# Decode attention on one core: K's sums all on DVE in blocks of 64 keys, V a head behind K

## The chip, the core and the metric

The kernel runs on one core of a Trainium2 chip. The metric is the device time of one execution in microseconds (us). Here it is the median of three runs, 1392.78 us (1392.25 to 1393.84). The profile is of one further execution.

The core has several engines that run side by side: PE (matrix multiply, TensorE), DVE (VectorE), ACT (ScalarE), POOL (GpSimd) and SP (SyncE, which here only issues DMA transfers). Transfers between the chip's main memory and the core's on-chip buffers are carried by 16 DMA engines, which all queues share. A tile lies across 128 partitions; PSUM is the memory that PE writes its results to.

## The reference

One token is decoded. It is normalised, goes through an attention over a cache of 16384 keys for each of 32 heads, and beside that through a gated feed-forward part:

```python
xn = _layernorm(x)                                   # x: 576 numbers
q = (xn @ wq) as 32 heads of 128
scores = einsum("bhqd,bhkd->bhqk", q, k_cache) * 128 ** -0.5
p = softmax(scores)                                  # over 16384 keys
o = einsum("bhqk,bhkd->bhqd", p, v_cache)
A = o as a row of 4096 @ wo
B = (gelu(xn @ w_gate) * (xn @ w_up)) @ w_down       # 4608 wide
return x + A + B
```

All is float32. One head's K is 16384 x 128 numbers, 8.39 MB, and its V the same, so that the 32 heads bring 537 MB; the weights wq, w_gate, w_up, w_down and wo bring some 51 MB more. Every byte is used once.

## The kernel before, in words

**Layout.** Partition p holds 128 keys of a head (R = 128) with 128 numbers each, so one head's K or V is one tile of 128x16384, 64 KB in each partition, loaded by one DMA from SP. Three such buffers, `slots` (L41), are all that fits; `slot()` (L57) hands them out in turn, and a load waits until the last reader of the tile that was there before is done. The loads of weights, K and V all go through `load` (L60), so they stand in SP's queue in the order of the program, and a load that waits holds up those behind it.

**Start.** One slot, `mix`, takes the tails of wq, w_gate and w_up and their fourth rows; wq has a slot of its own. `project` (L121) multiplies xn with a weight on PE, in four groups of partitions. `ffn` (L153) loads the rest of w_gate or w_up into a slot, projects, lets ACT copy the result into that slot's unused end (`gc`, L160), and four small DMAs from POOL's queue gather it into `gu` (L164). `ffn_act` (L171) then computes gelu(g) * u into `hT`, on DVE with one tanh on ACT; its last DVE operation (L181) waits for the gathers of w_up's part.

**A head.** `q_spread` (L143) puts the head's q on all partitions. `qk` (L192) does 16 keys of every partition at a time, 8 times: DVE multiplies K in place with q (L198), DVE then sums 10 of the 16 keys' products (L202), and ACT sums the other 6, each with one activation that also accumulates (L201, which the profile shows as an ACTIVATE and a READ_ACCUMULATOR). `softmax` (L204) finds the largest score: a maximum on DVE (L206), a transpose on PE (L208), a maximum on DVE again (L210), a matmul that puts it on all partitions (L212); ACT then takes exp (L216). `pv` (L218) multiplies V with the probabilities in 32 matmuls of four keys, which the profile shows as 64; the four keys' results stand in four rows and four blocks of PSUM, of which only the matching ones (row r, block r) are wanted. `out_a` (L225) picks these on DVE, with a multiplication by a mask in PSUM (L227) and a sum (L229), and `out_b` (L231) sums the partitions on PE (L233). The picking for head h-1 stands behind the fourth block of head h.

**Order of the loads.** K0, V0, K1, V1 and so on through the three slots. So K of head h+1 takes the slot of V of head h-1 and waits for its PV; V of head h takes the slot of K of head h-1 and waits for its sums. Between engines the order is set by a scheduler that goes by the program's order where the program does not pin it with `keep_in_program_order`.

**End.** w_down comes in pieces of 28 and 8 rows of 576 numbers per partition (L265, L266), wo in pieces of 20, 6, 3, 2 and 1 rows (L267 to L271). The attention output is divided by the sums of exp and gathered into `oT` by a DMA (L289). `add_out` (L255) multiplies each row of w_down with hT and each row of wo with oT, accumulating in PSUM (L258); from row 26 of wo on (MERGE) two of the four partial sums are folded into the other two (L303, L305). Then x is added (L309) and the result stored (L310).

Of the kernel before, what the change touches and what calls it, by code (L numbers as in the profile page):

```python
# [16 lines left out]
R = SK // P  # L17
SUB = 16
NSUB = R // SUB
N_ACT = 6  # L20
SLOTS = 3
DJ = 4
# [4 lines left out]
HD = H * DH  # L27
QG, QB = HD // 4, 512
FG, FB = DF // 4, 384
WD_T = DF // P  # L30
WO_T = HD // P
WD_PIECES = (28, 8)
WO_PIECES = (20, 6, 3, 2, 1)
MERGE = 26
# [3 lines left out]
def kernel(ctx: ExitStack, tc: tile.TileContext, x, k_cache, v_cache, wq, wo, wg, wu, wd, out):  # L38
    nc = tc.nc
    cpool = ctx.enter_context(tc.tile_pool(name="cpool", bufs=1))  # L40
    slots = ctx.enter_context(tc.tile_pool(name="slots", bufs=SLOTS))  # L41
    spool = ctx.enter_context(tc.tile_pool(name="spool", bufs=2))
# [13 lines left out]

    def slot():  # L57
        return slots.tile([P, R * DH], F32, tag="s", name="slot")

    def load(dst, src):  # L60
        nc.sync.dma_start(dst, src)
        return dst

    mix, wq_t = slot(), slot()
    at = 0

    def part_of_mix(src):
        nonlocal at
        n = src.shape[1]
        at += n  # L70
        return load(mix[:, at - n : at], src)

    ROW3 = 3 * DF
    tails = {"q": part_of_mix(wtail["q"])}
    load(wq_t, wmain["q"])
    row3 = {}
    for n in "gu":
        row3[n] = part_of_mix(wmain[n][:, ROW3:])
        tails[n] = part_of_mix(wtail[n])

# [26 lines left out]
    for j in range(DJ):  # L107
        nc.tensor.matmul(px[:, j : j + 1], xm[:, j, :], ones[:1, :1], start=True, stop=True)
    xd = cpool.tile([1, D - DM, 2], F32, name="xd")
    nc.vector.tensor_copy(xd, xrow[:, DM:].unsqueeze(2).to_broadcast([1, D - DM, 2]))  # L110
# [24 lines left out]

    steps = [(DJ, tails["q"])] + [(j, wq_t[:, j * HD : (j + 1) * HD]) for j in range(DJ)]
    pq = project(steps, QG, QB)
# [15 lines left out]
    def ffn(which):  # L153
        n = "gu"[which]
        t = slot()
        steps = [(3, row3[n]), (DJ, tails[n])]
        for j in range(DJ - 1):
            lo, hi = j * DF, (j + 1) * DF
            steps.append((j, load(t[:, lo:hi], wmain[n][:, lo:hi])))
        gc = t[:, ROW3 : ROW3 + FG]  # L160
        pg = project(steps, FG, FB)
        nc.scalar.activation(gc.rearrange("p (b f) -> p b f", f=FB), pg, AF.Copy)
        for q in range(4):
            nc.gpsimd.dma_start(gu[32 * q : 32 * q + 32, which, :], gc[32 * q : 32 * q + 1, :])  # L164
# [22 lines left out]

    S, PE_, KT, VT, OM = {}, {}, {}, {}, {}
    lsum = cpool.tile([P, H], F32, name="lsum")
    oall = cpool.tile([P, H], F32, name="oall")  # L190

    def qk(h, i):  # L192
        kt = KT[h].rearrange("p (n d) -> p n d", d=DH)
        if i == 0:
            S[h] = spool.tile([P, R], F32, name="s")
        lo, nv = i * SUB, SUB - N_ACT
        blk = kt[:, lo : lo + SUB, :]
        nc.vector.tensor_mul(blk, blk, Q[h].to_broadcast([P, SUB, DH]))  # L198
        for n in range(nv, SUB):
            jk = spool.tile([P, DH], F32, name="jk", bufs=1)  # L200
            nc.scalar.activation(jk, blk[:, n, :], AF.Copy, accum_out=S[h][:, lo + n : lo + n + 1])  # L201
        nc.vector.tensor_reduce(S[h][:, lo : lo + nv], blk[:, :nv, :], axis=AX.X, op=ALU.add)  # L202

    def softmax(h):  # L204
        pm = spool.tile([P, 1], F32, name="pm")
        nc.vector.reduce_max(pm, S[h], axis=AX.X)  # L206
        pt = ps_s.tile([P, 512], F32, tag="sm", name="pt")
        nc.tensor.transpose(pt[:1, :P], pm, ident)  # L208
        nm = spool.tile([1, 1], F32, name="nm")
        nc.vector.tensor_reduce(nm, pt[:1, :P], axis=AX.X, op=ALU.max, negate=True)  # L210
# [5 lines left out]
        nc.scalar.activation(PE_[h], S.pop(h), AF.Exp, bias=nb, scale=SCALE, accum_out=lsum[:, h : h + 1])  # L216

    def pv(h):  # L218
        vt, pe = VT.pop(h), PE_.pop(h)
        for k in range(0, R, 4):  # L220
            q = 32 * (k // 4 % 4)
            nc.tensor.matmul(PO[h % 2][q : q + 4, :], pe[:, k : k + 4], vt[:, k * DH : (k + 4) * DH],  # L222
                             start=k < 16, stop=k >= R - 16)
# [12 lines left out]
    q_spread(0)  # L236
    for h in range(H):
        KT[h] = load(slot(), kv[h])
        VT[h] = load(slot(), vv[h])
        for i in range(NSUB):  # L240
            qk(h, i)
            if h == 0 and i == 3:
                ffn_act()
            if h > 0 and i == 3:
                out_a(h - 1)
                out_b(h - 1)
        KT.pop(h)
        softmax(h)
        if h + 1 < H:
            q_spread(h + 1)  # L250
        pv(h)

# [8 lines left out]

    wd0, wd1, wo1 = slot(), slot(), slot()
    a, b = WD_PIECES
    n0 = WO_PIECES[0]
    load(wd0[:, : a * D], wdv[:, : a * D])  # L265
    load(wd1[:, : b * D], wdv[:, a * D :])  # L266
    load(wd1[:, b * D : (b + n0) * D], wov[:, : n0 * D])  # L267
    lo = n0
    for n in WO_PIECES[1:]:
        load(wo1[:, (lo - n0) * D : (lo + n - n0) * D], wov[:, lo * D : (lo + n) * D])  # L270
        lo += n  # L271
    wd_rows = [wd0[:, j * D : (j + 1) * D] for j in range(a)] + [wd1[:, j * D : (j + 1) * D] for j in range(b)]
    wo_rows = [wd1[:, (b + j) * D : (b + j + 1) * D] for j in range(n0)]
    wo_rows += [wo1[:, j * D : (j + 1) * D] for j in range(WO_T - n0)]

    out_a(H - 1)
    out_b(H - 1)
    pl = ps_s.tile([P, 512], F32, tag="sm", name="pl")
# [14 lines left out]

    x2 = wo1[:, R * DH - 2 * HALF : R * DH - HALF]
# [3 lines left out]
    part = wo1[:, R * DH - HALF :]  # L298
    nc.vector.memset(part, 0.0)
# [39 lines left out]
```

## Time and profile before

| | us |
|---|---|
| median of three runs (lowest, highest) | 1392.78 (1392.25, 1393.84) |
| the profiled execution | 1390.13 |
| its span, first to last instruction | 1388.4 |
| DVE busy | 990.0 |
| ACT busy | 653.6 |
| PE busy | 415.1 |
| mean rate of all transfers | 424 GB/s |

The span is what the views of the profile cover. The execution's own time lies 1.73 us over it. Times in the views are in us from the span's start. A row of a group of instructions reads: line, engine, operation, tile written, tile read, shapes, count, then the busy time in us and the mean of one in ns, then how long the engine stood idle just before them and for whom. A row of a window reads: its bounds and length, the busy us and count of PE, PE's weight load, DVE, ACT and POOL in turn, then the clock that PE was granted (1.00 is full), the busy share of the 16 DMA engines and the GB/s. A row of the chain reads start, length and what it was. The queues q8 and q14 carry the engines' own instructions, q1 the data.

### The profile page before, as it was taken

Reading aid. Unit: us, or ns where it says so; the run is one execution under the profiler, and the core shown is the slowest. Engines: PE = TensorE matmul, PEld = TensorE weight load, DVE = VectorE, ACT = ScalarE, POOL = GpSimd, SP = SyncE. Lnnn points to the kernel's source line nnn. Section 1 sums busy time; section 2 is a strip of 40 time slices with the busy share of each in tenths; the row PEclk is TensorE's granted clock in tenths of the full one; section 3 lists DMA queues with packets and bytes.
Section 4 is the critical chain, followed back from the end, with each engine's and each line's share of the span. In section 5 each row is a group of like instructions: output and inputs, shape, how many; then the busy total and the mean of one; then the engine's idle time right before and its main releaser. Section 6 shows DMA issues by size and latency. Waiting matters only on the chain.

```text
span 1388.4 us, 10333 instructions
## 1 busy us (share of the span) xinstructions
PE 415.1 (30%) x2881; PEld 113.9 (8%) x2881; DVE 990.0 (71%) x668; ACT 653.6 (47%) x3240; POOL 6.3 (0%) x17
## 2 busy tenths in 40 slices
PE   4511323333332122333231123333321223232317
PEld 1100000000000000000000000000000000000002
DVE  1008888777777887777777887777778887777770
ACT  0105555545454555445445555454545554454450
POOL 0000000000000000000000000000000000000000
PEclk9855565565655556565655665656555565656559
DMA  9999999999999999999999999999999999999996
GB/s 400 431 416 427 439 433 431 435 429 443 427 424 448 423 429 435 423 424 429 431 429 418 433 425 420 431 427 422 427 422 429 434 429 427 427 422 422 424 412 296
DMA packets 12367, 588.31 MB, mean 424 GB/s; under 512 B 1667, under 2 KB 1685, under 8 KB 2070
## 3 DMA queue, kind: packets, MB, share of 16 engines
q1 hardware_dynamic: 11956, 587.60, 98.9%
q8 instruction: 22, 0.36, 0.1%
q14 instruction: 35, 0.29, 0.1%
q0 software_dynamic: 352, 0.06, 0.0%
q10 hardware_dynamic: 2, 0.00, 0.0%
HBM read 587.60 MB, written 0.00 MB: 423 GB/s over the span
## 4 chain that ended last, share of the span: by engine, by line
DMA 49%; DVE 34%; PE 13%; ACT 4%; issue 1%; SPq 0%; POOL 0%; DVEq 0%; ACTq 0%
DMA slot<-in_A_k_cache_dram 41%; DVE slot L198 20%; DVE s L202 11%; PE po L222 10%; DMA slot<-in_B_w_up_dram 3%; ACT jk L201 3%; DMA slot<-in_A_wo_dram 2%; DMA slot<-in_A_wq_dram 2%; DMA gu<-slot 1%; PE pg L132 1%; DVE po L227 1%; DVE om L229 1%; PE acc L258 1%; ACT pe L216 1%; PE pt L208 0%
## 5 line engine op out<-in xcount | busy, mean ns | idle before, releaser
L201 ACT ACTIVATE jk<-slot 128x128 f32<-128x128 f32 x1536 | 475.0, 309 | 552.1 <-DVE slot L198 509.7
L198 DVE TENSOR_TENSOR slot<-slot,qs 128x2048 f32<-128x2048 f32 x256 | 576.4, 2283 | 211.2 <-DMA slot<-in_A_k_cache_dram 211.2
L202 DVE TENSOR_REDUCE s<-slot 128x10 f32<-128x1280 f32 x256 | 370.2, 1477 | 1.1
L222 PE MATMUL po<-slot,pe 128*4 128x512 f32 x2048 | 294.0, 738 | 14.8 <-ACT pe L216 14.5
L201 ACT ACTIVATION_READ_ACCUMULATOR jk<-slot 128x1 f32 x1536 | 286.4, 186 | 0.0
L208 PE MATMUL pt<-ident,pm 128*1 128x128 f32 x32 | 11.9, 373 | 460.9 <-DVE pm L206 460.9
L233 PE MATMUL pc<-ones,om 128*128 128x1 f32 x64 | 18.6, 359 | 438.2 <-DVE om L229 438.2
L222 PEld LDWEIGHTS po<-slot,pe 128*4 128x4 f32 x2048 | 54.5, 98 | 233.8 <-issue 209.7
L233 PEld LDWEIGHTS pc<-ones,om 128*128 128x128 f32 x64 | 15.8, 308 | 467.9 <-DVE om L229 467.9
L174 DVE TENSOR_TENSOR t<-gu 128x36 f32<-128x36 f32 x1 | 0.2, 196 | 65.1 <-DMA gu<-slot 65.1
L132 PE MATMUL pg<-slot,xnb 128*32 128x384 f32 (+1 forms) x256 | 31.5, 643 | 32.6 <-DMA slot<-in_A_wq_dram 13.2
L208 PEld LDWEIGHTS pt<-ident,pm 128*1 128x1 f32 x32 | 2.5, 79 | 464.8 <-DVE pm L206 411.1
L206 DVE TENSOR_REDUCE pm<-s 128x1 f32<-128x128 f32 x32 | 9.1, 286 | 36.7 <-ACT jk L201 36.7
L214 ACT ACTIVATE nb<-pb 128x1 f32<-128x1 f32 x32 | 5.5, 171 | 57.6 <-PE pb L212 57.6
L227 DVE TENSOR_TENSOR po<-po,sel 128x512 f32<-128x512 f32 x32 | 22.0, 688 | 11.3 <-PE po L222 11.3
L147 PE MATMUL pq<-qrow,ones 1*128 1x128 f32 x64 | 24.9, 489 | 0.0
L212 PE MATMUL pb<-nm,ones 1*128 1x1 f32 x64 | 17.7, 343 | 14.8 <-DVE nm L210 14.8
L229 DVE TENSOR_REDUCE om<-po 128x128 f32<-128x512 f32 x32 | 21.8, 682 | 0.0
L181 DVE SCALAR_TENSOR_TENSOR hT<-t,gu 128x36 f32<-128x36 f32 x1 | 0.2, 197 | 28.3 <-DMA gu<-slot 28.3
L210 DVE TENSOR_REDUCE nm<-pt 1x1 f32<-1x128 f32 x32 | 8.9, 279 | 15.0 <-PE pt L208 15.0
L212 PEld LDWEIGHTS pb<-nm,ones 1*128 1x128 f32 x64 | 15.9, 306 | 23.3 <-issue 22.6
L234 ACT ACTIVATE oall<-pc 128x1 f32<-128x1 f32 x32 | 5.5, 171 | 22.6 <-PE pc L233 22.6
(61 smaller groups left out, 116.6 us busy)
## 6 DMA issues: line engine op xcount, KB each, us to landing
slot<-in_B_w_gate_dram SPq DMA_DIRECT2D x4, 2304.0 KB, 44.4
slot<-in_B_w_up_dram SPq DMA_DIRECT2D x4, 2304.0 KB, 35.2
slot<-in_B_w_down_dram SPq DMA_DIRECT2D x1, 8064.0 KB, 35.6
slot<-in_A_wo_dram SPq DMA_DIRECT2D x1, 5760.0 KB, 26.7
slot<-in_B_w_down_dram SPq DMA_DIRECT2D x1, 2304.0 KB, 13.1
slot<-in_A_wo_dram SPq DMA_DIRECT2D x1, 1728.0 KB
slot<-in_B_w_gate_dram SPq DMA_DIRECT2D x1, 1152.0 KB
slot<-in_B_w_up_dram SPq DMA_DIRECT2D x1, 1152.0 KB, 39.4
```

Source lines behind the costliest of these rows:

```text
L132: nc.tensor.matmul(pg[32 * q : 32 * q + 32, b, :size], lhs, rhs[:, lo : lo + size], start=k == 0, stop=k == len(steps) - 1)
L147: nc.tensor.matmul(pq[:, :DH], ones[r : r + 1, :], qrow[r : r + 1, lo : lo + DH], start=True, stop=True)
L198: nc.vector.tensor_mul(blk, blk, Q[h].to_broadcast([P, SUB, DH]))
L201: nc.scalar.activation(jk, blk[:, n, :], AF.Copy, accum_out=S[h][:, lo + n : lo + n + 1])
L202: nc.vector.tensor_reduce(S[h][:, lo : lo + nv], blk[:, :nv, :], axis=AX.X, op=ALU.add)
L208: nc.tensor.transpose(pt[:1, :P], pm, ident)
L212: nc.tensor.matmul(pb[:, :1], ones[:1, :], nm, start=True, stop=True)
L216: nc.scalar.activation(PE_[h], S.pop(h), AF.Exp, bias=nb, scale=SCALE, accum_out=lsum[:, h : h + 1])
L222: nc.tensor.matmul(PO[h % 2][q : q + 4, :], pe[:, k : k + 4], vt[:, k * DH : (k + 4) * DH], start=k < 16, stop=k >= R - 16)
L227: tc.keep_in_program_order(nc.vector.tensor_mul(o4, o4, sel.unsqueeze(2).to_broadcast([P, 4, DH])))
L229: nc.vector.tensor_reduce(OM[h], o4.rearrange("p r d -> p d r"), axis=AX.X, op=ALU.add)
L233: nc.tensor.matmul(pc[:, :1], OM.pop(h), ones[:, :1], start=True, stop=True)
```

## The change

Six things change together.

1. The three common slots become two for K (`kpool`) and one for V (`vpool`). `kslot()` and `vslot()` take the place of `slot()`.
2. V is loaded a head behind K: SP's order is K0, K1, V0, K2, V1 and so on. PV and the output of head h-1 stand behind the sums of head h. The last V takes a slot of K.
3. `qk` does 64 keys at a time, twice a head, and DVE sums all of them; ACT sums none. DVE's products and maxima are pinned to the program's order.
4. `out_a` and `out_b` become `out_head`: ACT copies the PSUM tile to the on-chip buffer, and four matmuls with the mask's columns both pick the wanted blocks and sum the partitions.
5. At the start wq's tail goes into w_gate's slot, w_gate and wq have K's two slots, w_up takes wq's, and the copies `gc` and `xd` go into `mix`. So K0 waits for the matmuls of w_gate and no longer for its gathers; V0 waits for all gathers.
6. At the end wo comes in pieces of 8, 6, 6, 6, 3, 2 and 1 rows: the first three in the slot with w_down's second piece, the rest in the third slot.

```diff
-SUB = 16
-NSUB = R // SUB
-N_ACT = 6
-SLOTS = 3
+SUB = 64
...
-WO_PIECES = (20, 6, 3, 2, 1)
+WO_PIECES = (8, 6, 6, 6, 3, 2, 1)
+WO_A = 20
...
-    slots = ctx.enter_context(tc.tile_pool(name="slots", bufs=SLOTS))
+    kpool = ctx.enter_context(tc.tile_pool(name="kpool", bufs=2))
+    vpool = ctx.enter_context(tc.tile_pool(name="vpool", bufs=1))
...
+    wq_t, wg_t, mix = kslot(), kslot(), vslot()
+    qt = load(wg_t[:, ROW3 : ROW3 + QS], wtail["q"])
     load(wq_t, wmain["q"])
...
     def ffn(which):
         n = "gu"[which]
-        t = slot()
+        t = kslot() if which else wg_t
...
-        gc = t[:, ROW3 : ROW3 + FG]
+        gc = mix[:, ROW3 + which * FG : ROW3 + (which + 1) * FG]
...
-        lo, nv = i * SUB, SUB - N_ACT
-        blk = kt[:, lo : lo + SUB, :]
-        nc.vector.tensor_mul(blk, blk, Q[h].to_broadcast([P, SUB, DH]))
-        for n in range(nv, SUB):
-            jk = spool.tile([P, DH], F32, name="jk", bufs=1)
-            nc.scalar.activation(jk, blk[:, n, :], AF.Copy, accum_out=S[h][:, lo + n : lo + n + 1])
-        nc.vector.tensor_reduce(S[h][:, lo : lo + nv], blk[:, :nv, :], axis=AX.X, op=ALU.add)
+        blk = kt[:, i : i + SUB, :]
+        tc.keep_in_program_order(nc.vector.tensor_mul(blk, blk, Q[h].to_broadcast([P, SUB, DH])))
+        nc.vector.tensor_reduce(S[h][:, i : i + SUB], blk, axis=AX.X, op=ALU.add)
...
-    def out_a(h):
-        o4 = PO[h % 2].rearrange("p (r d) -> p r d", d=DH)
-        tc.keep_in_program_order(nc.vector.tensor_mul(o4, o4, sel.unsqueeze(2).to_broadcast([P, 4, DH])))
-        OM[h] = spool.tile([P, DH], F32, name="om")
-        nc.vector.tensor_reduce(OM[h], o4.rearrange("p r d -> p d r"), axis=AX.X, op=ALU.add)
-
-    def out_b(h):
+    def out_head(h):
+        o4 = spool.tile([P, 512], F32, name="o4", bufs=1)
+        nc.scalar.activation(o4, PO[h % 2], AF.Copy)
         pc = ps_s.tile([P, 512], F32, tag="sm", name="pc")
-        nc.tensor.matmul(pc[:, :1], OM.pop(h), ones[:, :1], start=True, stop=True)
+        for j in range(4):
+            nc.tensor.matmul(pc[:, :1], o4[:, j * DH : (j + 1) * DH], sel[:, j : j + 1], start=j == 0, stop=j == 3)
         nc.scalar.activation(oall[:, h : h + 1], pc[:, :1], AF.Copy)
...
-    for h in range(H):
-        KT[h] = load(slot(), kv[h])
-        VT[h] = load(slot(), vv[h])
-        for i in range(NSUB):
-            qk(h, i)
-            if h == 0 and i == 3:
-                ffn_act()
-            if h > 0 and i == 3:
-                out_a(h - 1)
-                out_b(h - 1)
-        KT.pop(h)
-        softmax(h)
+    for h in range(H + 1):
+        if h < H:
+            KT[h] = load(kslot(), kv[h])
+        if h > 0:
+            VT[h - 1] = load(vslot() if h < H else kslot(), vv[h - 1])
+        if h < H:
+            for i in range(0, R, SUB):
+                qk(h, i)
+            KT.pop(h)
+        if h == 0:
+            ffn_act()
+        if h > 0:
+            pv(h - 1)
+            out_head(h - 1)
         if h + 1 < H:
             q_spread(h + 1)
-        pv(h)
+        if h < H:
+            softmax(h)
```

In the changed kernel's own order on DVE, `ffn_act` still stands ahead of head 0's products, as it does before.

More of the change, by code (lines that the diff above doesn't have):

```diff
@@ L28 @@
 QG, QB = HD // 4, 512
+QS = HD // 2
 FG, FB = DF // 4, 384
@@ L55, with kslot, vslot @@
     wdv = wd.rearrange("(p t) f -> p (t f)", t=WD_T)
-    def slot():
-        return slots.tile([P, R * DH], F32, tag="s", name="slot")
+    def kslot():
+        return kpool.tile([P, R * DH], F32, tag="k", name="kslot")
+    def vslot():
+        return vpool.tile([P, R * DH], F32, tag="v", name="vslot")
     def load(dst, src):
@@ L134, in project @@
         return pg[:, : group // size, :size]
-    steps = [(DJ, tails["q"])] + [(j, wq_t[:, j * HD : (j + 1) * HD]) for j in range(DJ)]
+    steps = [(DJ, qt)] + [(j, wq_t[:, j * HD : (j + 1) * HD]) for j in range(DJ)]
     pq = project(steps, QG, QB)
@@ L186 @@
         nc.vector.memset(z, 0.0)
-    S, PE_, KT, VT, OM = {}, {}, {}, {}, {}
+    S, PE_, KT, VT, OS = {}, {}, {}, {}, {}
     lsum = cpool.tile([P, H], F32, name="lsum")
@@ L260, in add_out, with load_rows @@
             seen.add(q)
-    wd0, wd1, wo1 = slot(), slot(), slot()
+    def load_rows(t, at, src, lo, n):
+        load(t[:, at * D : (at + n) * D], src[:, lo * D : (lo + n) * D])
+        return [t[:, (at + j) * D : (at + j + 1) * D] for j in range(n)]
+    ta, tb, te = vslot(), kslot(), kslot()
     a, b = WD_PIECES
[L264 to L270, printed above, removed]
-        lo += n
[L272 to L277, printed above, removed]
+    wd_rows = load_rows(ta, 0, wdv, 0, a) + load_rows(tb, 0, wdv, a, b)
+    wo_rows, lo = [], 0
+    for n in WO_PIECES:
+        wo_rows += load_rows(tb, b + lo, wov, lo, n) if lo < WO_A else load_rows(te, lo - WO_A, wov, lo, n)
+        lo += n
     pl = ps_s.tile([P, 512], F32, tag="sm", name="pl")
@@ L297 @@
         nc.gpsimd.dma_start(x2[32 * i : 32 * i + 1, :], xf[:, i * HALF : (i + 1) * HALF])
-    part = wo1[:, R * DH - HALF :]
+    part = te[:, R * DH - HALF :]
     nc.vector.memset(part, 0.0)
```

23 lines of the change are left out of this document (8 added, 15 removed).

## The prediction

> **What bounds the kernel now.** I read the page first: the busy shares and the queues.
>
> ```profile
> span 1388.4 us, 10333 instructions
> PE 415.1 (30%) x2881; PEld 113.9 (8%) x2881; DVE 990.0 (71%) x668; ACT 653.6 (47%) x3240; POOL 6.3 (0%) x17
> ...
> q1 hardware_dynamic: 11956, 587.60, 98.9%
> q8 instruction: 22, 0.36, 0.1%
> q14 instruction: 35, 0.29, 0.1%
> ```
>
> No engine is near full; the transfers are. K and V are 64 loads of 8.39 MB, 537 of 587.60 MB, and no edit takes a byte away. So I ask whether the 98.9% is all moving bytes, and took windows by stage, then two by single loads (V29, K31), then the chain's K loads (start, length) and their issues.
>
> ```profile
> 153.77:522.00 368.23, 103.31 (x646) 28.90 (x646) 289.94 (x191) 192.07 (x960) 0.00 (x0) 0.60 1.00 432
> 522.00:1309.50 787.50, 217.23 (x1420) 56.08 (x1420) 613.98 (x400) 403.89 (x2020) 0.00 (x0) 0.61 1.00 427
> ...
> 1230.50:1250.70 20.20, 9.45 (x64) 1.72 (x64) 14.02 (x8) 9.39 (x48) 0.00 (x0) 0.67 1.01 423
> 1290.40:1309.80 19.40, 1.75 (x7) 1.11 (x7) 16.57 (x13) 10.69 (x55) 0.00 (x0) 0.50 1.00 433
> ```
> ```profile
> 35.95 40.24 DMA slot<-in_B_w_up_dram
> 83.25 19.55 DMA gu<-slot
> 103.05 33.54 DMA slot<-in_A_k_cache_dram
> 257.53 34.14 DMA slot<-in_A_k_cache_dram
> 1278.99 36.74 DMA slot<-in_A_k_cache_dram
> ```
>
> The last two numbers of a window are the DMA share and GB/s. The share is 1.00 in all, yet late V loads run at 423, K loads at 433: some packets take longer. By landings: K1, the third load, lands at 103.05 + 33.54 = 136.59; K5, the eleventh, at 291.67; K31, the 63rd, at 1315.73. That is 155.1/8 = 19.39 us a load early and 1024.1/52 = 19.69 later. The 52 later loads lose 0.3 us each, **16 us**; K1 to K31, 60 loads, takes 1179.1 where 60 x 19.39 = 1163.1.
>
> Where does it come from? Small packets (under 512 B) are one per engine and load. I looked at them round the end of K5 (landing 291.67) and of K31 (1315.73):
>
> ```profile
> DMA packets 43, 1.77 MB, mean 553 GB/s; under 512 B 16, under 2 KB 16, under 8 KB 16
> DMA packets 46, 2.03 MB, mean 406 GB/s; under 512 B 15, under 2 KB 15, under 8 KB 15
> DMA packets 19, 1.13 MB, mean 452 GB/s; under 512 B 1, under 2 KB 1, under 8 KB 1
> ...
> 1307.60 0.33 SPq L61 DMA_DIRECT2D slot<-in_A_v_cache_dram  x1
> ```
>
> The windows are 288.5 to 291.7, 1308 to 1313 and 1313 to 1315.5. At K5 all 16 engines end within 3.2 us; at K31 fifteen have ended by 1313 and **one engine is some 3 to 5 us late**. A load lands with its last engine. V31, issued at 1307.60 when K31's slot of V came free, is there 8.1 us before K31 lands, but only about 2 to 3 before the fifteen want it. Its packets then start slowly. The late engine is never short of work, so it must carry more: the page's instruction queues are the only other traffic. ACT has 3240 of its instructions in the run and q14 brings 35 packets of 8 KB (0.29 MB): in the two stages
>
> ```profile
> q14 instruction: 10, 0.08, 0.1%
> q14 instruction: 22, 0.18, 0.1%
> ```
>
> that is 10 in 368.23 us and 22 in 787.50, about one a head. One such packet a head, on one engine, fits the 0.3 us a load (0.6 a head). That it falls on one engine, and is ACT's, is my reading; no row names an engine.
>
> **The Trainium skill** speaks against this: "Runtime: NRT & Kernel Launch", section "Instruction fetch mechanics", has each sequencer refill in 16 KiB blocks through its own DMA queue, "mostly hidden". By that rule fewer ACT instructions would give nothing; it is the second rival below. The trace agrees with the 16 KiB on q8, and has 8 KB on q14.
>
> **The change, part by part.** The groups and waits that price it:
>
> ```profile
> L201 ACT ACTIVATE jk<-slot 128x128 f32<-128x128 f32 x1536 | 475.0, 309 | 552.1 <-DVE slot L198 509.7
> L198 DVE TENSOR_TENSOR slot<-slot,qs 128x2048 f32<-128x2048 f32 x256 | 576.4, 2283 | 211.2 <-DMA slot<-in_A_k_cache_dram 211.2
> L202 DVE TENSOR_REDUCE s<-slot 128x10 f32<-128x1280 f32 x256 | 370.2, 1477 | 1.1
> L222 PE MATMUL po<-slot,pe 128*4 128x512 f32 x2048 | 294.0, 738 | 14.8 <-ACT pe L216 14.5
> ...
> L149 ACT ACTIVATE qs<-pq 128x128 f32<-128x128 f32 x32 | 8.3, 260 | 4.6 <-PE pq L147 4.6
> L139 ACT ACTIVATE qrow<-pg 128x1024 f32<-128x1024 f32 x1 | 1.0, 1023 | 31.2 <-PE pg L132 31.2
> ...
> L206 DVE TENSOR_REDUCE pm<-s 128x1 f32<-128x128 f32 x32 | 9.1, 286 | 36.7 <-ACT jk L201 36.7
> ...
> L210 DVE TENSOR_REDUCE nm<-pt 1x1 f32<-1x128 f32 x32 | 8.9, 279 | 15.0 <-PE pt L208 15.0
> ```
>
> *DVE.* Per head 16 operations become four of 128x8192. The reduces of 128 and 1280 elements give (1477 - 286)/1152 = 1.034 ns an element; 2048 takes 2283. So 8192 takes 8.6 to 8.7 us by the slope with its fixed 0.15, and at most 9.45 by the reduce's plain 1.154 ns. I take 8.65: 34.6 a head, with pm, nm and the 0.47 wait for PE (15.0/32) 35.7, at most 38.9. K comes every 2 x 19.39 = 38.8. DVE stays just under the transfers, and its idle 211.2 nearly goes; it costs nothing.
>
> *ACT* loses 96 instructions a head (1536 pairs) and gains the copy of PO, 128x512, which no row shows: between the 260 ns of 128x128 and the 1023 of 128x1024, say 0.6 us. 6 instructions a head stay. The DVE passes L227 and L229 go, and PE has four small matmuls for one. PV takes 294.0/32 = 9.2 us of a head's 38.8, and the next PV is the first to want PO or the copy's buffer. All this lies beside the transfers and costs nothing; if it took twice as long it would still fit.
>
> *Slots and queue.* SP now issues K0 K1 V0 K2 V1 and so on. K(h+2) waits for head h's last reduce: K(h) landing + 35.7, while its turn comes at + 58.2; 22 us of cover. V(h) waits for PV(h-1), some 9.2 to 9.8 us after V(h-1) landed; K(h+1) has then 9.3 us to go, against 8.1 at V31 now. Behind a waiting V stands K(h+2), which has the 22 us. If PV took over 17 us, V would be late.
>
> *Start.* K0 now needs only wg's matmuls, not the gathers:
>
> ```profile
> 61.77 1.13 ACT L162 ACTIVATE slot<-pg 128x1152 f32<-128x1152 f32 x1 [20.78 <-PE pg L132]
> 73.62 0.33 SPq L61 DMA_DIRECT2D slot<-in_A_k_cache_dram  x1
> 102.92 0.20 DVE L181 SCALAR_TENSOR_TENSOR hT<-t,gu 128x36 f32<-128x36 f32 x1 [28.31 <-DMA gu<-slot]
> ...
> 0.74 0.51 ACTq L82 DMA_DIRECT2D xrow<-in_A_x_dram  x1
> 2.59 0.74 DVE L97 BATCH_NORM_STATS2 st<-xrow 1x6 f32<-1x288 f32 x2
> ...
> slot<-in_A_k_cache_dram SPq DMA_DIRECT2D x1, 24.1
> ```
>
> K0 was issued at 73.62 and landed 24.1 later, 97.7: 21.5 after w_up (76.19), not 19.4. Issued at 62 it saves 2: K0, K1, V0 end at 76.2 + 58.2 = 134.4. But DVE's order still has hT, which waits for the gathers (19.55, to 102.8), ahead of head 0's products. So qk(0) runs from 103.1 to 137.7, and K2 waits for it: issued 137.9, first bytes about 2 us on (estimate, from xrow's load issued at 0.74 and used at 2.59), end 139.9 + 19.4 + 0.5 = **159.8**. A hole of 5 us that now isn't there (bounds: 5 to 8 by DVE's two rates). The fourth load now lands at 136.59 + 19.4 = 156.0: **+3.8**. Head 1 ends at 173.7, K3's turn is at 179.2: no second hole.
>
> *60 loads* up to V31 at 19.39, as ACT's fetches are gone: 1163.1, and 2 for what q8 still spreads (my choice, nearer to K5's 3.2 than to nothing). The bounds are 1163.1 and the 1179.1 of now; I take the low side because the early stage, with no engine late, ran at it for eight loads on end. V31 lands at 159.8 + 1165.1 = 1324.9; now at 1315.73 + 19.5 = 1335.2.
>
> *Tail.*
>
> ```profile
> 1348.00:1356.00 8.00, 6.84 (x38) 1.69 (x42) 0.23 (x1) 0.67 (x3) 0.00 (x0) 0.55 0.93 357
> 1360.38 0.94 SPq L61 DMA_DIRECT2D slot<-in_A_wo_dram  x2
> slot<-in_A_wo_dram SPq DMA_DIRECT2D x1, 288.0 KB, 21.6
> 1374.40 6.53 PE acc L258 x104
> 1382.12 2.93 PE acc L258 x24
> ```
>
> The last piece is issued about 1360.85 and lands at 1382.45, 47.2 after V31; the span ends 6.0 later. Of the 47.2, 8 x (1 - 357/432) = 1.4 is w_down's late second piece, which will be early (its slot, K31's, comes free 22 us ahead of its turn); 2 I add, since now the one late engine makes up some of its lag in the small last pieces, and a lag that isn't there can't be made up. Of the 6.0, rows 0 to 25 of wo (6.53) stood ready only with the piece of 20; in pieces of 8, 6 and 6 they start as they land (two more DMAs at 0.47 of SP each, long before their turn), and after the last piece one row (4/24 x 2.93 = 0.5) is left instead of most of 2.93: -2.0. End: 1324.9 + 47.8 + 4.0 = **1376.7** against 1388.4, **-11.7**. The profiled execution took 1390.13, 1.73 over its span, and the median of the runs, 1392.78, is 2.65 over that: 1376.7 + 4.4 = **1381**.
>
> **Rivals.**
> 1. *DVE takes over* (slower). If a long operation takes over (38.8 - 1.1)/4 = 9.4 us, DVE sets the pace. At 9.8 (1.2 ns an element) the last head's sums end at 103 + 32 x 40.3 = 1393, and PV, wo's matmuls and the end behind them (9.2 + 6.5 + 2.9 + 3.5) come after that: about 1415. For: 9.45 is the upper bound above. Against: the two rates from long rows, 1.03 to 1.115. Chance 0.08.
> 2. *The late engine stays* (the fetches aren't ACT's, or cost nothing): the 60 loads gain nothing; +3.8 - 1.4 - 2.0 = +0.4: 1393. For: no row names the engine. Against: it grows with q14's beat. Chance 0.13.
> 3. *The wait for PV takes the place of the wait for DVE:* V is late for the fifteen engines again after some heads, so half of the 16 is kept: 1381 + 7 = 1388. Chance 0.10.
> 4. *No hole at K2*, or no lag at all: 1381 - 6 = 1375. Chance 0.05.
>
> **How the numbers follow.** My forecast has 0.64, its own range 1376 to 1387. The range 1374 to 1393 takes in rivals 3, 4 and about half of 2, and leaves out 1. About 0.2% (2.8 us) is what a measurement of this kernel can tell from no change. Faster by more: 0.64 + 0.10 + 0.05 = 0.79; within: rival 2's 0.13; slower: rival 1's 0.08.
>
> **What would show it.** q14 falls from 35 packets to under 12; late windows run at 432 like early ones; the sixteen small packets at a late K stay within 4 us; SP waits for DVE once at 137.9 with a dip in GB/s there; DVE's long operations take 8.65; the last PE group after wo has a few matmuls. It is wrong if one engine is still late with q14 gone, or V's issue comes after K's fifteen.

## The result, and the profile after

The changed kernel takes **1378.71 us** in the median of four runs (1377.55 to 1379.76), the kernel before 1392.94 beside it (1392.25 to 1393.84): a ratio of **0.9897** (95% interval 0.988 to 0.9914), 14.2 us. The forecast was 1381.0, faster. The profiled execution took 1378.02, 1.8 over its span of 1376.2.

The page of the changed kernel, its busy shares and queues:

```profile
span 1376.2 us, 6971 instructions
...
PE 432.8 (31%) x3073; PEld 136.0 (10%) x3073; DVE 1134.4 (82%) x220; ACT 61.4 (4%) x200; POOL 6.3 (0%) x17
...
q1 hardware_dynamic: 12244, 587.60, 98.9%
q8 instruction: 24, 0.39, 0.1%
...
q14 instruction: 5, 0.04, 0.0%
```

DVE is up by 144 us of busy time and the kernel is faster; ACT has a tenth of its work left; q14 fell from 35 packets to 5. The same stretches as before, and the one round K2's issue ahead of them (the last two numbers of a window are the DMA share and GB/s):

```profile
134.00:148.00 14.00, 9.82 (x63) 2.35 (x67) 13.37 (x5) 0.67 (x3) 0.00 (x0) 0.62 0.78 315
153.77:522.00 368.23, 103.89 (x696) 32.86 (x696) 349.11 (x61) 16.07 (x57) 0.00 (x0) 0.61 1.00 432
522.00:1309.50 787.50, 234.87 (x1564) 72.80 (x1568) 714.57 (x122) 34.22 (x120) 0.00 (x0) 0.61 1.00 433
```

The late stretch runs like the early one, 433 GB/s where it had been 427. The first window is the price: a share of 0.78. The timelines of SP's issues and of DVE show why:

```profile
63.38 17.22 SPq L64 DMA_DIRECT2D kslot<-in_A_k_cache_dram  x2
101.55 0.33 SPq L64 DMA_DIRECT2D vslot<-in_A_v_cache_dram  x1
136.58 0.33 SPq L64 DMA_DIRECT2D kslot<-in_A_k_cache_dram  x1
148.95 0.33 SPq L64 DMA_DIRECT2D vslot<-in_A_v_cache_dram  x1
```
```profile
101.59 0.20 DVE L177 SCALAR_TENSOR_TENSOR hT<-t,gu 128x36 f32<-128x36 f32 x1 [25.37 <-DMA gu<-vslot]
101.82 8.69 DVE L193 TENSOR_TENSOR kslot<-kslot,qs 128x8192 f32<-128x8192 f32 x1
...
127.87 8.69 DVE L194 TENSOR_REDUCE s<-kslot 128x64 f32<-128x8192 f32 x1
```

K2 goes out at 136.58, when head 0's last reduce is done, and that head began only behind hT. The three groups whose durations the forecast had to work out:

```profile
L194 DVE TENSOR_REDUCE s<-kslot 128x64 f32<-128x8192 f32 x64 | 555.9, 8686 | 2.2
L193 DVE TENSOR_TENSOR kslot<-kslot,qs 128x8192 f32<-128x8192 f32 x64 | 555.8, 8685 | 72.3 <-DMA kslot<-in_A_k_cache_dram 72.3
...
L219 ACT ACTIVATE o<-po 128x512 f32<-128x512 f32 x32 | 19.1, 597 | 869.0 <-PE po L214 869.0
```

They are 8.69 us (8.65 was taken) and 0.6 us (0.6). The end, as the timeline of PE has it:

```profile
1363.17 3.06 PE L250 MATMUL acc<-kslot,oT 128*1 128x288 f32 x24 [2.51 <-DMA kslot<-in_A_wo_dram]
1367.33 1.64 PE L250 MATMUL acc<-kslot,oT 128*1 128x288 f32 x24 [1.10 <-DMA kslot<-in_A_wo_dram]
1369.55 0.65 PE L293 MATMUL acc<-kslot,ident 128*1 128x288 f32 x4 [0.58 <-DVE kslot L291]
1370.03 3.08 PE L250 MATMUL acc<-kslot,oT 128*1 128x288 f32 x24
```

PE now takes wo's rows as the pieces land, but behind the merge still stand 24 matmuls. (That the first of these groups takes 3.06 and the second 1.64 is the clock, the third number from the right in the window: 0.50 there, 1.00 from 1368 on.)

```profile
1364.00:1366.00 2.00, 2.00 (x20) 0.44 (x12) 0.00 (x0) 0.00 (x0) 0.00 (x0) 0.50 0.96 395
...
1368.00:1370.00 2.00, 1.42 (x20) 0.39 (x14) 0.46 (x1) 0.00 (x0) 0.00 (x0) 1.00 0.45 181
```

**One number more for all that follows.** Each load of K or V leaves 16 small packets, one per DMA engine, when an engine has done its share. From their times in the trace's packet records I take, for each V load from 300 us on, four things: the *spread* (first to last engine) of the K load that is in flight when V is issued; the *lead* (from SP's issue of V to the last engine's end of that K); the *margin* (from the issue to the first engine's end, that is, lead less spread); and the *loss* (how much later than 19.36 us after K's the middle engine ends V; a load is eight packets of 2.42 us on each engine, 19.36). V31 of the changed order is issued while K31 is in flight but stands behind V30; it is in the means of leads and margins with K31's end.

| kernel | lead | spread, mean (largest) | margin | loss per V load x count |
|---|---|---|---|---|
| before | 7.55 | 5.69 (6.6) | 1.86 | 0.55 x 26 |
| changed | 9.48 | 3.33 (5.1) | 6.15 | 0.02 x 27 |

The kernel before loses 14 us of its 1388 at these starts, the changed one half a microsecond. That is where the time came from: by the ends of the last engines, the last 60 loads took 1179.0 us before and take 1164.9 now. The hole at K2 takes 3.7 us back, and the tail gives 1.8.

### The profile page after: what moved, and what is told of

It is laid out like the page before. It is cut to its first block, busy times and chain, and to the rows that moved or that the text cites. A ratio compares the mean times of both kernels' runs of the same rounds, so it can differ in the third digit from the quotient of the medians.

```text
span 1376.2 us, 6971 instructions
## 1 busy us (share of the span) xinstructions
PE 432.8 (31%) x3073; PEld 136.0 (10%) x3073; DVE 1134.4 (82%) x220; ACT 61.4 (4%) x200; POOL 6.3 (0%) x17
## 4 chain that ended last, share of the span: by engine, by line
DMA 49%; DVE 48%; PE 2%; issue 0%; POOL 0%; SPq 0%; ACT 0%; DVEq 0%
DMA kslot<-in_A_k_cache_dram 37%; DVE s L194 24%; DVE kslot L193 24%; DMA kslot<-in_A_v_cache_dram 3%; DMA kslot<-in_B_w_up_dram 3%; DMA kslot<-in_A_wo_dram 2%; DMA kslot<-in_A_wq_dram 2%; DMA gu<-vslot 1%; PE pg L128 1%; PE po L214 1%; PE acc L250 0%; PE pt L200 0%; DVE pm L198 0%; POOL gu L160 0%; SPq L64 0%
## 5 line engine op out<-in xcount | busy, mean ns | idle before, releaser
L193 DVE TENSOR_TENSOR kslot<-kslot,qs 128x8192 f32<-128x8192 f32 x64 | 555.8, 8685 | 72.3 <-DMA kslot<-in_A_k_cache_dram 72.3
L194 DVE TENSOR_REDUCE s<-kslot 128x64 f32<-128x8192 f32 x64 | 555.9, 8686 | 2.2
L214 PE MATMUL po<-vslot,pe 128*4 128x512 f32 x1984 | 282.8, 734 | 596.0 <-DMA vslot<-in_A_v_cache_dram 595.2
L214 PEld LDWEIGHTS po<-vslot,pe 128*4 128x4 f32 x1984 | 54.6, 98 | 798.1 <-issue 797.2
L219 ACT ACTIVATE o<-po 128x512 f32<-128x512 f32 x32 | 19.1, 597 | 869.0 <-PE po L214 869.0
L222 PE MATMUL pc<-sel,o 128*128 128x1 f32 x256 | 33.7, 253 | 23.2 <-ACT o L219 23.2
L222 PEld LDWEIGHTS pc<-sel,o 128*128 128x128 f32 x256 | 31.0, 191 | 53.0 <-ACT o L219 53.0
L128 PE MATMUL pg<-kslot,xnb 128*32 128x384 f32 (+1 forms) x208 | 26.5, 664 | 30.1 <-DMA kslot<-in_B_w_gate_dram 14.0
L202 DVE TENSOR_REDUCE nm<-pt 1x1 f32<-1x128 f32 x32 | 8.9, 279 | 17.7 <-PE pt L200 17.7
L204 PE MATMUL pb<-nm,ones 1*128 1x1 f32 x64 | 17.7, 343 | 14.7 <-DVE nm L202 14.7
L250 PE MATMUL acc<-kslot,oT 128*1 128x288 f32 x128 | 11.5, 456 | 5.2 <-DMA kslot<-in_A_wo_dram 5.2
L208 ACT ACTIVATE pe<-s,nb 128x128 f32<-128x128 f32 x32 | 12.8, 401 | 1.2 <-ACT nb L206 0.2
L269 DVE RECIPROCAL rl<-pl 128x32 f32<-128x32 f32 x1 | 0.4, 358 | 14.2 <-PE pl L267 14.2
```

What stands on the lines that cost most here:

```text
L128: nc.tensor.matmul(pg[32 * q : 32 * q + 32, b, :size], lhs, rhs[:, lo : lo + size], start=k == 0, stop=k == len(steps) - 1)
L193: tc.keep_in_program_order(nc.vector.tensor_mul(blk, blk, Q[h].to_broadcast([P, SUB, DH])))
L194: nc.vector.tensor_reduce(S[h][:, i : i + SUB], blk, axis=AX.X, op=ALU.add)
L202: tc.keep_in_program_order(nc.vector.tensor_reduce(nm, pt[:1, :P], axis=AX.X, op=ALU.max, negate=True))
L219: nc.scalar.activation(o4, PO[h % 2], AF.Copy)
L222: nc.tensor.matmul(pc[:, :1], o4[:, j * DH : (j + 1) * DH], sel[:, j : j + 1], start=j == 0, stop=j == 3)
```

## The experiments

My theory at the start: ACT's instruction fetches make one DMA engine late, V is then issued too late for the other fifteen, and each V starts slowly. The rivals: the order of the loads gained it and the fetches cost nothing; or DVE's or PE's waits explain it. Unless said otherwise an edit is made to the changed kernel. Each run was compared with runs of the kernel before on the same chip, whose median lay between 1392.9 and 1394.5; so a difference between two experiments is good to some 1.5 us. First, fetches added, sums added and DVE's early work moved.

**act96: 96 more ACT instructions a head, behind the sums.**

```diff
         nc.vector.tensor_reduce(S[h][:, i : i + SUB], blk, axis=AX.X, op=ALU.add)
+        for _ in range(24):
+            jk = spool.tile([P, 1], F32, name="jk", bufs=1)
+            js = spool.tile([P, 1], F32, name="js", bufs=1)
+            nc.scalar.activation(jk, S[h][:, i : i + 1], AF.Copy, accum_out=js)
```

> The changed kernel with 48 pairs of small ACT instructions added to each head (each copies one column of the scores into a tile that nobody reads), so that ACT has about as many instructions as before, but no sums of K. My theory (the gain comes from ACT's instruction fetches, which made one DMA engine late): q14 comes back from 5 packets to about 30, one of the 16 engines falls behind by some 0.6 us a head, and the time rises by 10 to 16 us over the changed kernel's 1378.7, to 1389 to 1395. Rival (the gain comes from the order of the loads, with K and V issued earlier): no change, 1377 to 1381, all 16 engines within 5 us at the last loads.

Measured: 1392.32 (ratio to before 0.9988, 0.9978 to 0.9998), 29 packets in q14, 428 GB/s in the late window. **act48**, with half as many:

> The same with 24 pairs a head, half the dose. My theory: q14 at about 17 packets, the late engine loses 0.3 us a head, of which the spread of some 5 us that the changed kernel has anyway hides a part; 4 to 8 us over the changed kernel, 1382 to 1387. Rival (order of the loads): 1377 to 1381.

Measured: 1384.44 (0.9938, 0.9921 to 0.9955), 17 packets, 431 GB/s. Both agree with the theory, and neither proves it. The waits of act96 show another thing that it did:

```profile
DVE nm L206 <- PE pt L204: 116.1, 32, 3.9
```

The changed kernel has 17.7 us here, 0.6 a head; act48 has the same 116.1 as act96. The added instructions hold up the copy of PO on ACT, PE's matmuls behind it and so DVE, 3.6 us a head: 39.0 us of DVE a head, above the 38.8 that two loads take. So two causes could give this time, and the test was made anew with instructions that nothing waits for:

**act96b: 96 more, behind the exponentials.**

```diff
             q_spread(h + 1)
+            for _ in range(48):
+                jk = spool.tile([P, 1], F32, name="jk", bufs=1)
+                js = spool.tile([P, 1], F32, name="js", bufs=1)
+                nc.scalar.activation(jk, Q[h + 1][:, 0, :1], AF.Copy, accum_out=js)
```

> The changed kernel with 96 more small instructions a head on ACT (48 pairs of a 128x1 copy and its accumulator read, results unused); nothing is left out. Unlike in the run with 96 behind the sums, they read the next head's spread query and stand behind the exponentials, so that no sum of DVE should wait for them: DVE's wait for PE ahead of L206's second reduce should be back at 1 us a head or less, and a head's DVE work at about 36 us. My theory (ACT's instruction fetches make one of the 16 DMA engines late, 0.3 us a load) expects q14 at 25 to 35 packets, one late engine and 428 GB/s or less in 522:1309.5, and 1388 to 1394. The rival (that run's 13 us came from DVE's longer cycle, 39.1 us a head, and not from the fetches) expects the changed kernel's 1377 to 1381 with 432 to 433 GB/s, whatever q14 carries.

Measured: **1391.29** (0.9984, 0.9974 to 0.9995), the same to a microsecond. Its waits, its queue, its late window, and the packets at the end of K31 (1286 to 1291.5, then to 1297):

```profile
DVE nm L202 <- PE pt L200: 17.7, 32, 0.6
```
```profile
q14 instruction: 28, 0.23, 0.0%
```
```profile
522.00:1309.50 787.50, 234.28 (x1540) 72.34 (x1540) 706.67 (x121) 312.60 (x2051) 0.00 (x0) 0.61 1.00 429
```
```profile
DMA packets 48, 2.16 MB, mean 393 GB/s; under 512 B 15, under 2 KB 15, under 8 KB 15
...
DMA packets 37, 2.36 MB, mean 429 GB/s; under 512 B 1, under 2 KB 1, under 8 KB 1
```

DVE's wait is that of the changed kernel to the digit; fifteen engines end early and one late. The packet records also settle what the prediction had to leave as a reading, on which engine the fetches fall. On each engine a packet starts within some ns of the end of the one ahead, so its packets can be followed one by one. From 280 us to V31's end q14 brings 24 packets, and 22 of them stand on the engine that ends its load last. Each takes 0.31 us, and the 64 KB packet behind it 2.8 instead of 2.42: one fetch puts that engine back by 0.7 us. The rival of DVE's longer cycle has fallen: ACT instructions that compute nothing, delay no sum and move 0.19 MB of instructions cost 12.6 us.

**act48b: half of that dose.** By now there were two readings of how a fetch costs.

```diff
-            for _ in range(48):
+            for _ in range(24):
```

> The changed kernel with 48 more small instructions a head on ACT (24 pairs, reading the next head's spread query; results unused, nothing left out): half the dose of the run with 96. Two readings of what a fetch costs. By the first, each fetch adds its share at once, so that half the fetches cost half: q14 at 16 to 18 packets, 430 or 431 GB/s in 522:1309.5, 1384 to 1387. By the second, fetches only make one engine late, by some 0.7 us each, and cost nothing until that lag has used up the time by which V is issued ahead (the lag of the run with 96 grew to 7 us by about 760 us, and only from there on were the other fifteen engines slow too): then 17 fetches make a lag of 4 to 6 us, 522:1309.5 stays at 432 or 433 GB/s, and only the end of V31 moves, by 1 to 3 us: 1379.5 to 1382.5.

Measured: **1382.43** (0.9919, 0.9906 to 0.9933).

```profile
q14 instruction: 16, 0.13, 0.0%
```
```profile
522.00:1309.50 787.50, 231.12 (x1542) 72.15 (x1545) 711.52 (x122) 169.26 (x1080) 0.00 (x0) 0.61 1.00 432
```

Half the fetches cost 3.7 us, not 6.3, and the late rate doesn't fall: the second reading. The spread shows both doses at one glance. Here it is that of every fourth head's V load; the columns are the times at which its middle engine ends, rounded, and all is in us:

| | 371 | 526 | 682 | 838 | 994 | 1150 | 1305 |
|---|---|---|---|---|---|---|---|
| changed | 2.0 | 2.0 | 3.3 | 3.6 | 3.6 | 3.6 | 5.1 |
| act48b | 2.3 | 3.7 | 5.0 | 5.7 | 6.9 | 8.2 | 6.8 |
| act96b | 3.5 | 5.6 | 7.6 | 7.2 | 7.9 | 7.8 | 7.9 |

The late engine falls back until the spread is some 8 us of the lead's 9.3 to 9.5; from there on V's start waits for it, and the others lose what it loses. act96b is there by 682, act48b only by 1150. Up to then a fetch costs nothing but the last landing.

**pool96: the same number of instructions on POOL.**

```diff
             q_spread(h + 1)
+            for _ in range(96):
+                jk = spool.tile([P, 1], F32, name="jk", bufs=1)
+                nc.gpsimd.tensor_copy(jk, Q[h + 1][:, 0, :1])
```

> The changed kernel with 96 small copies a head on POOL (128x1, results unused), which no other work waits for; nothing is left out. If any engine's instruction fetches make one DMA engine late, a queue of instructions carries 20 to 40 packets more, 522:1309.5 falls to 428 or 429 GB/s and the time is 1386 to 1395. If only ACT's do (POOL's fetches are spread over the engines, or POOL's work does not load the transfers), 1377 to 1382.

Measured: 1394.24 (1.0001, 0.9992 to 1.001). Its queue, and POOL's group:

```profile
q14 instruction: 29, 0.24, 0.0%
```
```profile
L244 POOL COPY jk<-qs 128x1 f32<-128x1 f32 x2976 | 1061.1, 357 | 289.5 <-ACT qs L145 107.7 <-POOL jk L244 0.2
```

It is the same queue number, with 24 packets more, and the late engine is there too (spread 8.7 at 858 us). So it isn't ACT alone that makes it late. The time is not clean: POOL ended its copies only at 1372 and issued oT's gather behind them, which alone puts the end back, and DVE waited 48.6 us in all for q's copy on ACT, which waited for POOL's copies, so they weren't as free as expected. What this run shows is the spread, and that V31's last engine ends at 1336.2 and not at 1324.2; at K2 it was 1.5 us behind.

**The other half: the order of the loads.** Two runs each undo one of the two large parts. **after_actsums** has the old sums with the new order:

```diff
-SUB = 64
+SUB = 16
+N_ACT = 6
...
+        for n in range(nv, SUB):
+            nc.scalar.activation(blk[:, n, :], blk[:, n, :], AF.Copy, accum_out=S[h][:, lo + n : lo + n + 1])
```

> The changed kernel with the sums of the kernel before: eight blocks of 16 keys, ten sums of each on DVE and six on ACT (the ACT passes write over their own keys); slots, order of loads, PV and tail stay as changed. If ACT's fetches are the cause, q14 is back at 30 or more packets, one DMA engine is late, 522:1309.5 falls to 427 or 428 GB/s and the time is 1385 to 1392, although V is loaded a head behind K. If the early issue of V and the order of the loads were what gained, it is 1372 to 1378, a little under the changed kernel, since head 0's products are through earlier and the hole ahead of K2 is smaller.

Measured: **1387.37** (0.9958, 0.9945 to 0.9971), as the theory has it.

```profile
q14 instruction: 32, 0.26, 0.0%
```
```profile
134.00:148.00 14.00, 9.84 (x66) 2.22 (x66) 14.00 (x10) 8.76 (x57) 0.00 (x0) 0.74 1.03 442
...
522.00:1309.50 787.50, 222.76 (x1540) 69.33 (x1540) 589.28 (x361) 332.17 (x2040) 0.00 (x0) 0.61 1.00 428
```

The fetches are back and the late rate is down to 428; the hole is gone, since ACT helps head 0 along. So the kernel to set beside it is ffn_late (below), which has no hole either and takes 1372.68: 14.7 us less. **old_order** has the new sums, picking and start of q with the three slots, the order K0 V0 K1 V1 and wo's pieces of before:

```diff
-    for h in range(H + 1):
-        if h < H:
-            KT[h] = load(kslot(), kv[h])
-        if h > 0:
-            VT[h - 1] = load(vslot() if h < H else kslot(), vv[h - 1])
+    for h in range(H):
+        KT[h] = load(slot(), kv[h])
+        VT[h] = load(slot(), vv[h])
```

> The sums of the changed kernel (two blocks of 64, all on DVE, PV blocks picked by PE) with the three slots and the order K0 V0 K1 V1 of the kernel before, and its pieces of wo. DVE needs 35.7 us a head, 3.1 under the 38.8 of two loads, so unlike in the kernel before with all sums in 16-key blocks it isn't the bound. V waits for the last reduce of the head before and is issued about 3 us before the K ahead of it lands. If only ACT's fetches cost, q14 has under 12 packets, the late stretch runs at 431 to 433 GB/s and the time is 1374 to 1381 (no hole of 5 us at K2 but 2 to 4 us more in the tail). If V's late issue costs by itself, each V starts slowly by 0.3 to 1 us, 420 to 428 GB/s with no single late engine, and the time is 1386 to 1405.

Measured: **1393.06** (0.9997, 0.9982 to 1.0012).

```profile
153.77:522.00 368.23, 104.45 (x693) 31.96 (x693) 330.03 (x57) 15.39 (x54) 0.00 (x0) 0.61 1.00 428
522.00:1309.50 787.50, 232.80 (x1540) 71.04 (x1540) 705.07 (x121) 34.19 (x120) 0.00 (x0) 0.60 1.00 427
```
```profile
q14 instruction: 5, 0.04, 0.0%
```

Here "only the fetches cost" falls: q14 has 5 packets, no engine is late, and nothing is gained. In this order V(h) waits for head h-1's last reduce, and DVE's 35.7 us a head leave only 4 us to K's landing. The loads are slow from the start, 428, and not only late. **before_dvesums** goes one step further back, the kernel before with all sums on DVE:

```diff
-N_ACT = 6
+N_ACT = 0
```

> The kernel before, with its three slots and its order of loads, but with all sums of K on DVE (16 keys at a time) and none on ACT: one part of the change alone. My theory, that both parts are needed: q14 falls under 14 packets and no engine falls behind, but V of head h waits for the sums of head h-1, which now take 35 to 37 us instead of 31, so V is issued only 2 to 3 us before it is wanted and starts slowly or late at every head: 0.3 to 1.5 us a head, 1386 to 1400. If fewer fetches are all that counts: 1379 to 1383. If the order of the loads is all that counts: not under 1393, and one engine late as before.

Measured: **1419.74** (1.0185, 1.0171 to 1.0198), 20 us above the upper end of what I expected.

```profile
L198 DVE TENSOR_TENSOR slot<-slot,qs 128x2048 f32<-128x2048 f32 x256 | 576.7, 2284 | 72.2 <-DMA slot<-in_A_k_cache_dram 55.4 <-ACT qs L149 16.8
L202 DVE TENSOR_REDUCE s<-slot 128x16 f32<-128x2048 f32 x256 | 575.3, 2279 | 1.1
...
L227 DVE TENSOR_TENSOR po<-po,sel 128x512 f32<-128x512 f32 x32 | 22.1, 690 | 11.1 <-PE po L222 11.1
L229 DVE TENSOR_REDUCE om<-po 128x128 f32<-128x512 f32 x32 | 21.9, 684 | 0.0
```

DVE has (576.7 + 575.3 + 22.1 + 21.9)/32 = 37.4 us a head, with the maxima and waits about 39, and V goes out 3 us before K lands. DVE still stands idle 55.4 us for K, so its own pace isn't the bound. By the packet records the V starts lose 27 us more than in the kernel before, of the 29 us between the two spans, and the K starts nothing. What DVE's longer work costs, it costs through the late issue of V. q14 has 9 packets and no engine is late, so it isn't the fetches.

**What a late issue costs.** All V loads from 300 us on of eight kernels that stand behind a K load, sorted by margin, whatever the cause:

| margin, us | loads | mean loss, us |
|---|---|---|
| under 0 | 6 | 1.51 |
| 0 to 1 | 32 | 1.09 |
| 1 to 1.5 | 25 | 0.73 |
| 1.5 to 2 | 33 | 0.47 |
| 2 to 2.5 | 16 | 0.14 |
| 2.5 to 3.5 | 15 | 0.05 |
| over 3.5 | 80 | 0.01 |

and by kernel:

| kernel | lead | spread, mean (largest) | margin | loss x count |
|---|---|---|---|---|
| act48b | 9.34 | 5.33 (8.2) | 4.01 | 0.00 x 27 |
| act96b | 9.29 | 6.76 (8.4) | 2.53 | 0.24 x 27 |
| after_actsums | 9.97 | 7.74 (9.2) | 2.23 | 0.32 x 26 |
| old_order | 4.12 | 2.50 (3.4) | 1.62 | 0.62 x 26 |
| before_dvesums | 2.94 | 2.47 (3.5) | 0.47 | 1.36 x 26 |
| sub16 (below) | 9.35 | 3.57 (5.2) | 5.77 | 0.01 x 27 |

A load issued about 2.2 us or more before the first engine wants it costs next to nothing; below that, each microsecond less costs the middle engine about half of one. Short lead (old_order) and long spread (act96b) come to the same. It accounts for most of act96b as well: the spans of the two profiled executions differ by 12.9 us, and V31's last engine ends at 1335.6 and not at 1324.2, 11.4 later. Of these, 6.0 are at the middle engine, nearly all lost at V's starts (0.24 x 27 = 6.5, against half a microsecond), and 5.4 are the last engine's lag behind it, 8.0 where the changed kernel has 2.6. The other 1.5 lie behind V31, and no run takes them apart.

**The small terms.** **ffn_late** moves gelu's DVE work, and so the wait for the gathers, behind head 2's products. It also pins these five DVE operations to the program's order:

```diff
-        if h == 0:
+        if h == 2:
             ffn_act()
```

> The changed kernel with the feed-forward's DVE operations moved from ahead of head 0's products to behind those of head 2. My theory: DVE starts on K0 when it lands, at about 96 instead of 102, K2 is issued at about 131 instead of 137, the hole in the transfers there (some 5 us) goes, and nothing takes it back: 1372.5 to 1375. Rival (the hole is made up for later, since all engines start level behind it): 1377 to 1380.

Measured: **1372.68** (0.9852, 0.9838 to 0.9865), as expected.

```profile
134.00:148.00 14.00, 10.78 (x74) 3.01 (x74) 13.97 (x2) 1.49 (x5) 0.00 (x0) 0.74 1.01 437
```
```profile
95.90 8.69 DVE L193 TENSOR_TENSOR kslot<-kslot,qs 128x8192 f32<-128x8192 f32 x1 [87.57 <-DMA kslot<-in_A_k_cache_dram]
```

Head 0 starts at 95.90 and not at 101.82, and the hole is closed: 6.0 us. **sub16** has eight blocks of 16 keys, all on DVE:

```diff
-SUB = 64
+SUB = 16
```

> The changed kernel with its sums in eight blocks of 16 keys instead of two of 64, still all on DVE. By the rows of the kernel before a product of 16 keys takes 2.28 us and a reduce of as many 0.15 + 1.034 x 2.048 = 2.27, so a head takes 36.4 + 1 and not 34.6 + 1: under the 38.8 of two loads. Theory: the block's size is of little weight, DVE's cover is K's 22 us; 1378 to 1381, q14 at 8 to 12 packets. Rival: 16 operations a head push DVE to the transfers' pace, K waits for DVE, and it is 1385 or more.

Measured: 1381.15 (0.9906, 0.9891 to 0.9921), with 433 GB/s late. Just over the theory's 1381, far from the rival's 1385: the transfers wait for DVE only at the start, where K2 is issued 3 us later:

```profile
139.63 0.33 SPq L64 DMA_DIRECT2D kslot<-in_A_k_cache_dram  x1
```

**wo_old** has wo's old pieces:

```diff
-WO_PIECES = (8, 6, 6, 6, 3, 2, 1)
+WO_PIECES = (20, 6, 3, 2, 1)
```

> The changed kernel with wo in the old pieces, 20, 6, 3, 2 and 1 rows. By the prediction the first 20 rows then stand ready only with the piece of 20, and PE has more left at the end: +2 us, 1380 to 1382. The rival: in the changed kernel 24 matmuls are left behind the merge anyway, since the merge waits for row 25, so the pieces gain nothing: 1378 to 1379.5.

Measured: 1381.12 (0.9907, 0.9892 to 0.9921), 2.4 us over the changed kernel.

```profile
1363.26 8.75 PE L250 MATMUL acc<-kslot,oT 128*1 128x288 f32 x104 [8.69 <-DMA kslot<-in_A_wo_dram]
1372.60 0.65 PE L293 MATMUL acc<-kslot,ident 128*1 128x288 f32 x4 [0.59 <-DVE kslot L291]
1373.08 3.08 PE L250 MATMUL acc<-kslot,oT 128*1 128x288 f32 x24
```

With one piece of 20 the merge comes at 1372.60, with three at 1369.55; the group behind it is the same 3.08. So the pieces gain ahead of the merge. **best_merge20** adds an earlier merge to ffn_late:

```diff
-MERGE = 26
+MERGE = 20
```

> The kernel with the pointwise work moved behind head 2's products (1372.7 before), and in addition the merge of the two pairs of partial sums after row 20 of wo and not row 26. If the 24 matmuls behind the merge are what keeps the end 2 to 3 us behind the last piece, one row instead of six is left there and the time falls by 1 to 2.5 us: 1370.5 to 1372. If the last piece's landing or the output's way to memory sets it, nothing changes: 1372 to 1374.

Measured: 1372.66 (0.985, 0.9834 to 0.9865), no change.

```profile
1360.87 0.65 PE L293 MATMUL acc<-kslot,ident 128*1 128x288 f32 x4 [0.58 <-DVE kslot L291]
1361.65 5.99 PE L250 MATMUL acc<-kslot,oT 128*1 128x288 f32 x48
```

Behind the merge all rows go to one pair of partial sums, and there a matmul takes 5.99/48 = 0.125 us; on two pairs in turn it is 1.64/24 = 0.068 (first window below), both at a granted clock of 1.00. So the 12 rows take 6 us and end when the old six did.

```profile
1353.00:1356.00 3.00, 1.64 (x24) 0.52 (x24) 0.00 (x0) 0.00 (x0) 0.00 (x0) 1.00 0.98 417
...
1364.00:1366.00 2.00, 2.00 (x19) 0.73 (x16) 0.00 (x0) 0.00 (x0) 0.00 (x0) 1.00 0.23 88
```
ffn_late is the best version, with or without this.

## Why the prediction was right, point by point

- **The late engine.** Right, with its cause: q14 fell to 5 packets, below the 12 named, the late windows run at 433, and act96b brings the loss back by instructions alone. Rival 2, that the late engine stays, has fallen. What the Trainium skill says in "Runtime: NRT & Kernel Launch", section "Instruction fetch mechanics", that the cost of crossing to the next block is "mostly hidden", can't be told from these rows for the engine that runs the instructions. For the transfers beside it, it doesn't hold: 12.6 us by act96b. Whether each sequencer has a queue of its own, as that section also says, these rows don't tell: ACT's 96 and POOL's 96 both stand under q14, but the packet records have q14's packets on more than one DMA engine (in act96b 22 on the last to end and 2 on others).
- **What of the change did it.** Half seen. I priced the removal of the fetches as if it were enough and checked the order of the loads only for harm. old_order shows that the sums alone give nothing: the long DVE work eats the lead (4.12 us where it was 7.55) as fast as the fetches give it back. The rest of the change without the sums gives 1387.37, with no hole at K2; with the sums it is 1378.71, and without the hole 1372.68. For the forecast it made no difference, since both were made.
- **The spread.** Said to stay within 4 us, was 5.1 at a late K. It is two groups of engines and no single one, and the lead of 9.5 (forecast 9.3) covers it, so it cost only the 2.6 us by which V31's last engine is behind the middle one. The 2 us that I left for q8 were a choice, but the packet records name q8 too: between 160 us and V31's end its 18 packets of 16 KB take 1.07 us each and the packet behind them 2.92 instead of 2.42, and they fall on different engines, only 4 of them on the last to end.
- **DVE, ACT, slots.** 8.69 for 8.65, 0.6 for 0.6; DVE's wait for K sums to 72.3 where it was 211.2. Rival 1 (9.4 us an operation) and rival 3 (V late behind PV; loss 0.02) have fallen. Rival 3's mechanism is real in old_order, by another wait.
- **Start and hole.** K0 issued at 63.38 (62), K2 at 136.58 (137.9), K2's last engine ends at 159.3 (159.8). The 2 us that I gave K2 to its first bytes are 1.9 in effect, but as 0.96 to the first packet and slow first packets. ffn_late confirms the price of the hole, 6.0 us, and rival 4's 1375 was what the kernel could have had.
- **60 loads.** From 159.3 to V31's last engine at 1324.2: 1164.9, against 1165.1. That it is so close is in part luck, since 2 us of it were a choice.
- **Tail.** From there to the end 52.0, against 51.8. The pieces of wo are worth 2.4 us by wo_old (2.0), but not by the step that I gave for it: I had one row left behind the last piece, and it is still 24 matmuls, because the merge waits for row 25. The gain comes from the rows ahead of it. The tail's other two terms, 1.4 less for w_down's piece and 2 more for the lag, no run takes apart.
- **From span to median.** I added 4.4 and it was 2.5. The profiled execution of before lay 2.65 under its median, that of the changed kernel 0.7 under its own; I had carried the 2.65 over. That is 1.9 of the 2.3 by which the forecast was high.

So the sum was right to a microsecond in the span (1376.2, forecast 1376.7), and of its terms none was off by more than 2.

## What to carry to other kernels

In a kernel bound by transfers, look at when each load is issued against when the *first* of the DMA engines runs out, not against when the load ahead lands; here 2.2 us of margin were enough, and each one missing cost about half a microsecond. Two things eat that margin, a late release of the buffer and a spread between the engines, and removing one while making the other worse gains nothing. Many small instructions on an engine that looks idle aren't free in such a kernel: here each fetch of 8 KB put one DMA engine back by 0.7 us, nearly always the one that was last already, and 23 more of them cost 12.6 us.

## What was not expected of the hardware

- **POOL's and DVE's instructions are fetched under the same queue number as ACT's.** 2976 more on ACT or POOL raised q14 from 5 packets to 28 or 29, 124 to 129 instructions to a packet of 8 KB; sub16's 384 more on DVE raised it from 5 to 8. So of the 30 packets that went with the change, some 3 or 4 are DVE's by this rate (668 instructions before, 220 now).
- **From issue to full speed** a load of 8.39 MB from SP takes about 2.2 us, as I estimate from the table of margins. The Trainium skill's page "DMA: Bandwidth & Descriptors", section "Specifications", gives about 0.6 us to the first byte on this path. The trace fits it, as far as the starts of packets show it: K2 of the changed kernel goes out to 16 idle engines, and its first packet starts 0.96 us after the issue's start, 0.63 after its end. But the sixteen first packets start over the next 0.8 us and take 3.1 us in the mean, where later ones take 2.42; for planning the issue the 2.2 counted.
- **The loss has a threshold.** 11 more fetches cost 3.7 us and 23 cost 12.6, since the spread first uses up spare lead.
- **PE on one pair of partial sums** takes 0.125 us a matmul of 288 columns at a granted clock of 1.00, on two pairs in turn 0.068, so that merging earlier gains nothing.
